# Another place of the heads in the transposed rows, merged early loads and another opening order in a retention + tanh-shrink kernel

## The chip, the cores and the metric

The kernel runs on one core of a Trainium2 chip. The metric is the device time of one execution in microseconds (us). Lower is better. The core has a matrix engine (TensorE, PE in the profile, with its weight loads as PEld), three engines for elementwise work (VectorE or DVE, ScalarE or ACT, GpSimd or POOL), and SyncE (SP), which here only issues DMAs. ScalarE can issue DMAs too. Each engine runs its own instructions in program order.

## The reference

Two blocks follow each other. The first is a recurrent retention over 4 batches, 8 heads, 768 tokens and head size 64, in float32:

```
gamma = 1 - 2 ** (-5 - arange(H));  scale = 1 / sqrt(D)
for t in range(S):
    state = gamma * state + outer(k[:, :, t], v[:, :, t])
    y[:, :, t] = scale * (q[:, :, t] @ state)
```

The second takes y as 3072 tokens of 512 features (8 heads x 64) and computes

```
h = x @ w_in            # 512 -> 2048
g = h - tanh(h)
out = g @ w_out         # 2048 -> 512
```

w_in and w_out come as float64 and are turned into float32 on the chip.

## The kernel before, in words

The 3072 tokens are 24 chunks of 128, six to a batch. A chunk ci passes these pieces, each with a letter in the order that is written out by hand (lines 891 to 912):

- Lk, Lq, Lv (`load_one`, line 245): the loads of its k, q and v, 256 KB each. The first eight chunks load q in another arrangement ("wide"), in two DMAs of 128 KB each (line 254). All go through SP's queue. There are two buffers for k, two for q, four for v, so a load waits until the earlier chunk in the buffer has been read.
- s, w (`scale`, line 266): q and v times powers of gamma, on VectorE (D) or POOL (P).
- t, T (`turn`, line 283): four transposes of k and four of q on TensorE into PSUM; c, C (`turn_copy`, line 301): ScalarE copies them out.
- p (`products`, line 331): 64x64 matmuls, k times v (line 342) and k times q (line 348); m (line 355): VectorE masks the scores; z, Z (lines 366 to 372): VectorE adds up the two states of the chunk.
- b (`outputs`, line 381), r: matmuls into the two y banks (line 397), b with the states and half of the masked scores, r with the other half; e (`see`, line 427): four tiny ScalarE reads between them; y (`keep_x`, line 443): ScalarE copies y into xT, the transposed rows that the second block uses as its input.

A 64x64 matmul uses one quarter of the array: a half of the rows (which half of the partitions it reads) and a half of the columns (which half it writes). Head h = 2p + i is pair p, member i. The place of its 64 output rows is set in `to_y`: before, the half of the columns is (i + p) % 2, the bank (ci + p) % 2. So in xT the heads of every second group of 128 rows stand swapped, and the rows of w_in are loaded in that order: in three DMAs (lines 126 to 135 and 159), one of 128 partitions and two of 64.

Weights come in 32 pieces of 512 KB (W): in each group of eight the first four are columns of w_in, the others rows of w_out. A piece is converted by A and l (ScalarE), D1 to D4 (VectorE), F and G (VectorE or POOL). The weights 3 to 8 are loaded into rooms that xT uses later.

The second block runs in steps of 256 tokens by 256 hidden features. A step has two halves of an up matmul (u, v; line 463), the activation (au, ath, aq0, aq1, alarge on ScalarE; f0 to f4 on VectorE) and a down matmul in two parts (o0, o1; line 530), with E for sums. The order covers chunks 0 to 7, weights 0 to 11 and steps 0 to 7. After it, loops run the remaining steps with the other chunks and weights between them; from the fifth group of 512 rows on by a form with fewer products (lines 668 and 777).

A piece "x:n" lets n dummy matmuls run ahead of the next TensorE group (`keep_busy`). Each engine and queue gets its instructions in the order in which the pieces are written, so a piece that waits holds up everything behind it on the same engine.

## Time and profile before

| | us |
|---|---|
| median of 4 runs (699.1 to 701.62) | 701.03 |
| profiled execution | 701.12 |
| its span | 699.3 |
| TensorE busy | 686.2 |
| VectorE busy | 520.0 |
| ScalarE busy | 433.2 |
| POOL busy | 350.3 |

The span goes from the first to the last instruction in the record; the execution's own time is 1.8 us longer. An engine counts as busy while one of its instructions runs. A line such as L342 is line 342 of the kernel. "A <- B x" in a table of waits says that A waited and B ended that wait. Idle time of an engine that is not the bottleneck costs nothing. The granted clock of TensorE was 1.00 throughout.

### The profile page before, as it was taken

How to read it: one execution, taken by the hardware profiler on the slowest of the kernel's cores; microseconds unless marked ns; L12 is line 12 of the kernel's file. 1: busy time of each engine (PE TensorE's matmuls, PEld its weight loads, DVE VectorE, ACT ScalarE, POOL GpSimd, SP SyncE). 2: the span in 40 equal slices, each digit the busy share in tenths (PEclk: the TensorE clock that was granted, in tenths of full speed). 3: DMA queues.
4: the chain of work that ended last, by engine and by line, in shares of the span. 5: the costliest groups of instructions: out<-in, count | busy, mean ns of one | idle time of the engine just before them, and what ended most of it. 6: DMA issues, size and time to landing. Idle time of an engine off the chain costs nothing.

```text
span 699.3 us, 16551 instructions
## 1 busy us (share of the span) xinstructions
PE 686.2 (98%) x6562; PEld 576.6 (82%) x6562; DVE 520.0 (74%) x893; ACT 433.2 (62%) x818; POOL 350.3 (50%) x518
## 2 busy tenths in 40 slices
PE   8889999999999999999999999999999999999997
PEld 7776666676767667789999999999999999999996
DVE  4787989988889865677776686676686676766765
ACT  4676777676866755565555665555566555566553
POOL 2352255554454685977854453354543444544333
PEclk9999999999999999999999999999999999999999
DMA  8883239878868666500000000000000000000001
GB/s 218 226 250 91 91 105 216 222 198 211 235 171 221 177 166 179 155 33 1 1 1 16 16 2 31 1 1 31 2 0 31 1 1 31 1 17 16 1 16 46
DMA packets 119677, 59.96 MB, mean 86 GB/s; under 512 B 101808, under 2 KB 112688, under 8 KB 119600
## 3 DMA queue, kind: packets, MB, share of 16 engines
q1 hardware_dynamic: 117008, 50.21, 27.9%
q10 hardware_dynamic: 2592, 8.69, 3.4%
q8 instruction: 52, 0.85, 0.5%
q14 instruction: 25, 0.20, 0.1%
HBM read 35.83 MB, written 14.68 MB: 72 GB/s over the span
## 4 chain that ended last, share of the span: by engine, by line
PE 92%; DMA 3%; DVE 1%; SPq 1%; issue 1%; ACT 1%; POOL 0%; POOLq 0%; DVEq 0%; ACTq 0%
PE h L777 28%; PE o L530 16%; PE h L463 15%; PE fast_t L668 10%; PE y L668 8%; PE fast_o L668 8%; PE y L397 3%; PE s L342 1%; PE s L348 1%; DMA raws<-in_moe_w_out_dram 1%; DMA k<-in_k_dram 1%; DMA v<-in_v_dram 1%; PE kqTp L297 1%; SPq L159 1%; SPq L254 0%
## 5 line engine op out<-in xcount | busy, mean ns | idle before, releaser
L476 ACT ACTIVATE th<-h 128x512 f32<-128x512 f32 x64 | 38.2, 597 | 142.2 <-DVE h L794 142.2
L619 POOL TENSOR_TENSOR s<-g 128x128 f32<-128x128 f32 x64 | 29.3, 457 | 191.5 <-DVE g L522 187.5
L463 PE MATMUL h<-xT,w 128*128 128x256 f32 x512 | 118.0, 382 | 0.0
L530 PE MATMUL o<-w,g 128*128 128x512 f32 x256 | 116.3, 596 | 0.0
L463 PEld LDWEIGHTS h<-xT,w 128*128 128x128 f32 x512 | 96.1, 190 | 22.2 <-issue 9.3
L530 PEld LDWEIGHTS o<-w,g 128*128 128x128 f32 x256 | 47.7, 190 | 46.5 <-issue 43.5
L777 PEld LDWEIGHTS h<-xT,w 128*128 128x128 f32 x512 | 76.8, 191 | 8.4 <-ACT fast_head L782 1.0
L522 DVE COPY_PREDICATED g<-large,th 128x512 f32<-128x512 int32 x88 | 72.3, 822 | 8.9
L777 PE MATMUL h<-xT,w 128*128 128x128 f32 x512 | 78.4, 276 | 0.2 <-ACT fast_head L782 0.2
L792 DVE TENSOR_TENSOR h<-h,fast_head 128x256 f32<-128x256 f32 x64 | 27.7, 432 | 67.7 <-PE h L777 65.1
L501 DVE TENSOR_TENSOR th<-h,th 128x512 f32<-128x512 f32 x88 | 60.1, 683 | 19.4 <-ACT th L474 18.2
L514 DVE SCALAR_TENSOR_TENSOR g<-q,h 128x512 f32<-128x512 f32 x64 | 44.1, 688 | 36.6 <-ACT q L490 35.3
L777 PE MATMUL h<-x,w 128*128 128x128 f32 x448 | 68.4, 275 | 0.0
L482 ACT ACTIVATE q<-u,tab 128x512 f32<-128x512 f32 x88 | 63.8, 725 | 1.7
L490 ACT ACTIVATE q<-u,tab 128x512 f32<-128x512 f32 x88 | 63.6, 723 | 0.0
L491 ACT ACTIVATE large<-u,tab 128x512 f32<-128x512 f32 x88 | 62.7, 712 | 0.0
L505 DVE SCALAR_TENSOR_TENSOR h<-q,h 128x512 f32<-128x512 f32 x88 | 60.8, 690 | 2.2 <-ACT q L482 2.2
L208 POOL TENSOR_TENSOR low<-low,power 128x512 f32<-128x512 f32 x25 | 32.5, 1298 | 56.6 <-DVE power L201 47.3
L777 PEld LDWEIGHTS h<-x,w 128*128 128x128 f32 x448 | 59.1, 192 | 0.0
L782 ACT COPY fast_head<-h 128x512 f32<-128x512 f32 x64 | 37.4, 585 | 19.5 <-PE h L777 18.8
L521 DVE TENSOR_TENSOR g<-g,u 128x512 f32<-128x512 f32 x64 | 48.0, 751 | 0.0
L787 POOL TENSOR_TENSOR fast_head<-fast_head 128x256 f32<-128x256 f32 x64 | 46.8, 731 | 1.5 <-ACT fast_head L782 1.5
(195 smaller groups left out, 1503.8 us busy)
## 6 DMA issues: line engine op xcount, KB each, us to landing
rows<-apart ACTq DMA_DIRECT2D x16, 512.0 KB, 4.2
k<-in_k_dram SPq DMA_DIRECT2D x24, 256.0 KB, 4.3
v<-in_v_dram SPq DMA_DIRECT2D x24, 256.0 KB, 5.7
raw<-in_moe_w_out_dram SPq DMA_DIRECT2D x12, 512.0 KB, 4.3
out_dram<-sum SPq DMA_DIRECT2D x22, 256.0 KB, 2.0
q<-in_q_dram SPq DMA_DIRECT2D x16, 256.0 KB, 4.7
raw<-in_moe_w_in_dram SPq DMA_DIRECT2D x14, 256.0 KB, 3.9
raw<-in_moe_w_in_dram SPq DMA_DIRECT2D x28, 128.0 KB, 4.0
```

The source lines that it names most:

```text
L463: nc.tensor.matmul(hp, w1[:, c, ts(2 * m2 + i, P)], xT[n // 2][:, c, ts(n % 2, TH)], start=(begins and c == 0), stop=(c == NC - 1), skip_g ...
L482: nc.scalar.activation(q0, shrinking[n, m2][0], AF.Square, bias=bias0)
L490: nc.scalar.activation(q1, u, AF.Square, bias=bias1, scale=math.sqrt(A))
L491: nc.scalar.activation(large, u, AF.Relu, bias=bias_m)
L501: nc.vector.tensor_tensor(th, hp, th, op=ALU.subtract)
L505: nc.vector.scalar_tensor_tensor(hp, in0=shrinking[n, m2][2], scalar=C0, in1=hp, op0=ALU.add, op1=ALU.mult)
L521: nc.vector.tensor_tensor(flat, src, u, op=ALU.mult)
L522: nc.vector.copy_predicated(flat, large.bitcast(I32), th)
L530: nc.tensor.matmul(o_p[j], gT[n, m2][:, i, ts(j, P)], w2[:, 2 * m2 + i], start=(first and i == 0), stop=(last and i == 1))
L668: nc.tensor.matmul(accs[n][k], left[k - 1], right, start=first and k in (1, 6, 7, 4), stop=last, skip_group_check=True)
L777: nc.tensor.matmul(hps[n, m2][:, ts(PLACE[k], P)], s_of[m2][k - 1][:, c], x_of[n][k - 1][:, c], start=(k == 1 and c == 0), stop=(c == 1), ...
L787: nc.gpsimd.tensor_tensor(odd_room[1], first[:, :2], first[:, 3:1:-1], op=ALU.add)
```

## The change

Four things change together.

1. The place of the heads: the half of the columns becomes p // 2, the bank (ci + i) % 2, the place in the bank p % 2. Every group of 128 rows in xT now holds one 64-row head of the first four and one of the last four, with no swap. The pieces of w_in are loaded in two DMAs of 64 partitions instead of three. The quarters of the array are walked in one fixed order, `QUARTERS`, in both parts of b and in r.
2. The wide q of the first eight chunks is loaded in one DMA of 256 KB instead of two of 128.
3. `load_one` takes a queue. Two loads, k of chunk 0 and q of chunk 1, are issued by ScalarE ("A" behind the number in the order).
4. The order of the opening is another: the loads of k, q and v of the first two chunks stand before weight 0, up steps come later, and other pieces are given to VectorE and POOL. The name of an o bank now carries n, since parts of different steps stand between each other.

```
--- before.py
+++ after.py
@@ -126,13 +126,8 @@
         f, r = divmod(i, 2 * NC)
         if r < NC:
             cols = ts(NC * f + r, P)
-            rows = w_in[:, cols].rearrange("(k two p) n -> p two k n", two=2, p=P)
-
-            return w1[:, :, cols], [
-                (ds(0, P), 0, rows[:, 0]),
-                (ds(0, D), 1, rows[D:, 1]),
-                (ds(D, D), 1, rows[:D, 1]),
-            ]
+            rows = w_in[:, cols].rearrange("(col c p) n -> col p c n", col=2, c=NC)
+            return w1[:, :, cols], [rows[0], rows[1]]
         m = NC * f + r - NC
         return w2[:, m], w_out[ts(m, P)]
 
@@ -155,8 +150,8 @@
             return
         if raw is not None:
             dst = raw.rearrange("p (c n) -> p c n", c=NC)
-        for r, k, w in src:
-            nc.sync.dma_start(out=dst[r, k::2], in_=w if raw is None else w.bitcast(U32))
+        for r, w in enumerate(src):
+            nc.sync.dma_start(out=dst[ts(r, D)], in_=w if raw is None else w.bitcast(U32))
 
 
 
@@ -242,7 +237,7 @@
     states = {}
     xT = {}
 
-    def load_one(ci, which):
+    def load_one(ci, which, queue=nc.sync):
         if ci >= NCH:
             return
         b, j = divmod(ci, CPB)
@@ -250,13 +245,12 @@
         t = inp.tile([P, H, D], F32, tag=nm, name=f"{nm}_{ci}", bufs=4 if nm == "v" else 2)
         rows = src[b, :, ts(j, P), :]
         if nm == "q" and ci < WIDE:
-            for i in range(2):
-                nc.sync.dma_start(
-                    out=t[:, ts(i, RUN)].rearrange("p r d -> p (r d)"),
-                    in_=rows[i::2].rearrange("g (p r) d -> p g (r d)", r=RUN),
-                )
+            queue.dma_start(
+                out=t.rearrange("p (i r) d -> p i (r d)", r=RUN),
+                in_=rows.rearrange("(g i) (p r) d -> p g i (r d)", i=2, r=RUN),
+            )
         else:
-            nc.sync.dma_start(out=t, in_=rows.rearrange("h p d -> p h d"))
+            queue.dma_start(out=t, in_=rows.rearrange("h p d -> p h d"))
         loaded.setdefault(ci, {})[which] = t
 
     def load_chunk(ci):
@@ -377,6 +371,7 @@
 
     y_banks = banks("y", "y").rearrange("p r (two n t) -> p two r n t", two=2, n=2)
     halfway = {}
+    QUARTERS = ((0, 0), (1, 1), (0, 1), (1, 0))
 
     def outputs(ci):
 
@@ -391,29 +386,24 @@
 
         def to_y(p, i, a, lhsT, rhs):
 
-            col, r = (i + p) % 2, (ci + p) % 2
+            col, r = p // 2, (ci + i) % 2
             start = (r, col) not in begun
             begun.add((r, col))
-            nc.tensor.matmul(y[ds(D * col, D), r, p // 2, ts(a, D)], lhsT, rhs,
+            nc.tensor.matmul(y[ds(D * col, D), r, p % 2, ts(a, D)], lhsT, rhs,
                              start=start, stop=True, skip_group_check=True)
 
         def intra(first):
-            for pp in range(NP // 2):
-                for i in range(2):
-                    for a in range(2):
-
-                        for col in range(2):
-                            p = 2 * pp + ((a + col) % 2 if first else (a + col + 1) % 2)
-                            if (i + p) % 2 != col:
-                                continue
-                            r = ds(D * a, D)
-                            to_y(p, i, a, vh[r, 2 * p + i], a_[r, i, p])
+            for odd in range(2):
+                for row, col in QUARTERS:
+                    p, i = 2 * col + odd, row if first else 1 - row
+                    r = ds(D * row, D)
+                    to_y(p, i, row, vh[r, 2 * p + i], a_[r, i, p])
 
         for a in range(2):
             if j or a:
-                for p in range(NP):
-                    for i in range(2):
-                        r = ds(D * i, D)
+                for odd in range(2):
+                    for i, col in QUARTERS:
+                        p, r = 2 * col + odd, ds(D * i, D)
                         to_y(p, i, a, st[r, a, p], qT[r, p, ts(a, D)])
         intra(True)
         halfway[ci] = intra
@@ -425,7 +415,7 @@
         for col in range(2):
             for r in range(2):
                 nc.scalar.copy(out=seen[ds(D * col, D), r : r + 1],
-                               in_=y[ds(D * col, D), r, 1, ds(D * ((ci + r + col) % 2), 1)])
+                               in_=y[ds(D * col, D), r, 1, ds(D * ((ci + r) % 2), 1)])
 
     def outputs_rest(ci):
         halfway.pop(ci)(False)
@@ -524,10 +514,10 @@
     def down(n, m2, j, first, last):
 
         if first:
-            o_p[j] = bank("o", f"o_{n}_{m2}_{j}")
-            keep_busy(o_p[j][:, :P])
+            o_p[n, j] = bank("o", f"o_{n}_{m2}_{j}")
+            keep_busy(o_p[n, j][:, :P])
         for i in range(2):
-            nc.tensor.matmul(o_p[j], gT[n, m2][:, i, ts(j, P)], w2[:, 2 * m2 + i],
+            nc.tensor.matmul(o_p[n, j], gT[n, m2][:, i, ts(j, P)], w2[:, 2 * m2 + i],
                              start=(first and i == 0), stop=(last and i == 1))
 
     def add_up(n, m2, j):
@@ -537,11 +527,11 @@
                 sums[i] = [op.tile([P, 2, DM], F32, tag="sum", name=f"sum_{i}"), set()]
         o, begun = sums[n][0][:, j], sums[n][1]
         if j in begun:
-            nc.vector.tensor_tensor(o, o_p[j], o, op=ALU.add)
+            nc.vector.tensor_tensor(o, o_p[n, j], o, op=ALU.add)
         elif done and j % 2:
-            nc.vector.tensor_copy(o, o_p[j])
+            nc.vector.tensor_copy(o, o_p[n, j])
         else:
-            nc.scalar.copy(out=o, in_=o_p[j])
+            nc.scalar.copy(out=o, in_=o_p[n, j])
         begun.add(j)
         if done:
             nc.sync.dma_start(out=rows_of(n)[:, j], in_=o)
@@ -853,11 +843,11 @@
             nc.vector.copy_predicated(gT[at_].rearrange("p i t -> p (i t)"),
                                       early[s, "large"].bitcast(I32), early[s, "th"])
 
-    engines = {"D": nc.vector, "P": nc.gpsimd}
+    engines = {"D": nc.vector, "P": nc.gpsimd, "A": nc.scalar}
     pieces = {
-        "Lk": lambda c: load_one(c, 0),
-        "Lq": lambda c: load_one(c, 1),
-        "Lv": lambda c: load_one(c, 2),
+        "Lk": lambda c, e=nc.sync: load_one(c, 0, e),
+        "Lq": lambda c, e=nc.sync: load_one(c, 1, e),
+        "Lv": lambda c, e=nc.sync: load_one(c, 2, e),
         "W": load_weights,
         "s": lambda c, e: scale(c, 0, e),
         "w": lambda c, e: scale(c, 1, e),
@@ -889,26 +879,26 @@
     if w_out.dtype != F32:
         rooms += [xp.tile([P, 2, 2 * BANK], U32, tag="xT", name=f"raws_{i}") for i in range(3)]
     order = """
-    Lk:0 Lq:0 Lv:0 x:9 t:0 s:0D Lq:1 x:3 T:0 W:0 w:0D Lk:1 c:0 C:0 A:0 x:2 p:0 z:0 Lv:1 m:0
-    Z:0 s:1P Lq:2 D1:0 D2:0 w:1D T:1 b:0 Lk:2 Lv:2 t:1 C:1 l:0 e:0 c:1 D3:0 r:0 x:2 p:1 W:1
-    D4:0 y:0 t:2 c:2 z:1 s:2P T:2 Lk:3 w:2P C:2 m:1 Z:1 b:1 p:2 e:1 r:1 F:0D A:1 G:0D D1:1 y:1
-    D2:1 z:2 Lq:3 Lv:3 Z:2 D3:1 l:1 W:2 s:3P x:1 t:3 w:3P u:0 m:2 Lq:4 c:3 T:3 s:4P C:3 D4:1
-    b:2 p:3 F:1D e:2 r:2 l:2 A:2 G:1D v:0 z:3 m:3 D1:2 y:2 Lv:5 Z:3 au:0 Lk:4 D2:2 D3:2 t:4
-    Lv:4 T:4 Lq:5 b:3 Lk:5 w:4P w:5D W:3 c:4 D4:2 F:2D C:4 e:3 W:4 W:5 ath:0 r:3 y:3 aq0:0
-    aq1:0 p:4 f0:0 z:4 m:4 Z:4 l:3 f1:0 A:3 alarge:0 u:2 G:2P t:5 s:5P T:5 v:2 D1:3 b:4 D2:3
-    D3:3 D4:3 A:4 c:5 F:3P f2:0 C:5 l:5 ath:2 Lq:6 Lk:6 Lv:6 W:7 e:4 G:3P Lq:7 W:8 W:9 p:5
-    au:2 Lv:7 r:4 aq0:2 y:4 A:5 aq1:2 l:4 f3:0 u:1 f0:2 m:5 z:5 f4:0 s:6P t:6 W:6 w:6P T:6
-    Lk:7 W:10 v:1 W:11 s:7P b:5 f1:2 f2:2 f3:2 c:6 C:6 au:1 p:6 e:5 D1:5 D1:4 D2:5 D2:4 r:5
-    D3:5 aq1:1 alarge:2 alarge:1 aq0:1 ath:1 u:3 D3:4 D4:5 v:3 D4:4 F:5P z:6 m:6 F:4D Z:6 f0:1
-    G:4D au:3 T:7 G:5P t:7 f1:1 A:6 y:5 c:7 f2:1 D1:6 o1:0 f4:2 w:7P C:7 b:6 D2:6 f3:1 p:7
-    aq0:3 e:6 ath:3 r:6 l:6 v:4 u:4 D3:6 m:7 f0:3 f1:3 D4:6 z:7 F:6P G:6P y:6 l:7 alarge:3
-    aq1:3 f2:3 f3:3 A:7 D1:7 b:7 f4:1 o0:0 A:11 e:7 D2:7 D3:7 D4:7 F:7P G:7D u:5 r:7 v:5 o1:1
-    o0:1 ath:4 au:4 aq0:4 l:11 f0:4 f4:3 f1:4 l:9 aq1:4 f2:4 f3:4 D1:11 E1:1 alarge:4 A:9 D1:9
-    D2:9 D2:11 D3:9 E0:1 y:7 ath:5 au:5 aq0:5 aq1:5 alarge:5 o1:2 v:7 D3:11 D4:11 o0:2 o1:3
-    D4:9 u:7 F:9D G:9P f0:5 o0:3 f1:5 F:11D f2:5 f3:5 f4:4 f4:5 G:11P A:8 D1:8 D2:8 E1:3 D3:8
-    Z:7 au:7 l:8 A:10 D1:10 D4:8 l:10 aq1:7 D2:10 F:8D D3:10 ath:7 f0:7 aq0:7 E0:3 D4:10 u:6
-    v:6 o0:4 au:6 o1:4 F:10P f1:7 f2:7 ath:6 alarge:7 G:10P f0:6 aq1:6 aq0:6 f1:6 alarge:6
-    o0:5 o1:5 E0:5 f3:7 f2:6 Lv:8 f3:6 f4:7 f4:6 Lk:8 Lq:8 W:12 W:14 W:13 G:8P E1:5
+    Lq:0 Lv:0 s:0P Lk:0A w:0D Lq:1A x:9 t:0 T:0 Lk:1 C:0 c:0 x:2 p:0 s:1P Lv:1 t:1 T:1 Lq:2
+    z:0 m:0 Z:0 Lv:2 C:1 W:0 w:1D c:1 b:0 Lk:2 Lq:3 x:1 p:1 s:2D e:0 z:1 m:1 r:0 y:0 Z:1 A:0
+    T:2 l:0 x:1 b:1 x:1 t:2 C:2 e:1 D1:0 c:2 D2:0 w:2P D3:0 Lk:3 Lv:3 x:1 p:2 r:1 D4:0 s:3P
+    m:2 y:1 z:2 t:3 Z:2 T:3 W:1 C:3 c:3 b:2 Lq:4 F:0P G:0P e:2 A:1 W:3 Lk:4 w:3D p:3 z:3 D1:1
+    r:2 y:2 l:1 Z:3 m:3 D2:1 u:0 D3:1 b:3 D4:1 e:3 Lv:4 F:1D s:4P r:3 T:4 A:3 x:1 t:4 G:1D v:0
+    Lq:5 D1:3 D2:3 y:3 c:4 C:4 l:3 w:4D p:4 D3:3 W:2 Lv:5 D4:3 Lk:5 s:5P z:4 m:4 au:0 ath:0
+    u:2 Z:4 Lq:6 T:5 F:3P w:5P W:4 aq0:0 v:2 A:2 Lv:6 t:5 C:5 D1:2 G:3P aq1:0 alarge:0 Lk:6
+    Lq:7 W:5 c:5 b:4 f0:0 p:5 D2:2 f1:0 D3:2 l:2 s:6P f2:0 D4:2 e:4 A:4 f3:0 m:5 D1:4 r:4
+    ath:2 v:1 z:5 t:6 au:2 T:6 aq0:2 aq1:2 c:6 y:4 l:4 F:2P C:6 G:2P u:1 A:5 Lk:7 W:7 Lq:8 W:6
+    w:6P f0:2 W:8 D2:4 Lv:7 f1:2 D3:4 s:7P f2:2 b:5 p:6 f4:0 f3:2 W:9 D1:5 W:10 D4:4 e:5 D2:5
+    F:4P W:11 z:6 m:6 r:5 Z:6 u:3 au:1 D3:5 alarge:2 aq0:1 D4:5 l:5 aq1:1 F:5D ath:1 T:7 G:4D
+    A:6 l:6 t:7 c:7 y:5 G:5D f0:1 v:3 f1:1 f4:2 f2:1 ath:3 f0:3 o1:0 au:3 C:7 f3:1 D1:6 D2:6
+    D3:6 o0:0 b:6 w:7P aq1:3 e:6 aq0:3 alarge:1 f1:3 D4:6 p:7 m:7 F:6P r:6 f2:3 v:4 alarge:3
+    y:6 u:4 A:7 au:4 z:7 f3:3 G:6D D1:7 f4:1 D2:7 D3:7 D4:7 b:7 u:5 v:5 A:9 l:7 F:7D G:7D e:7
+    r:7 o1:1 aq0:4 aq1:4 ath:4 A:8 D1:9 E1:1 o0:1 o0:2 au:5 l:9 D2:9 D3:9 f0:4 f1:4 f2:4 f3:4
+    D4:9 D1:8 f4:3 aq1:5 E0:1 alarge:4 y:7 ath:5 D2:8 D3:8 f4:4 F:9D G:9P f0:5 l:8 aq0:5 o1:2
+    D4:8 F:8P u:7 o0:3 f1:5 A:10 G:8P D1:10 f2:5 A:11 f3:5 v:7 au:7 D2:10 D1:11 o1:3 E0:3
+    D3:10 aq0:7 ath:7 l:10 D4:10 f0:7 f1:7 D2:11 F:10D E1:3 alarge:5 f4:5 D3:11 v:6 G:10D u:6
+    aq1:7 alarge:7 au:6 aq0:6 D4:11 f2:7 f3:7 f4:7 aq1:6 ath:6 o0:4 l:11 F:11P f0:6 f1:6
+    alarge:6 Z:7 f2:6 f3:6 f4:6 o1:4 o0:5 o1:5 Lk:8 Lv:8 W:12 W:13 W:14 E0:5 G:11P E1:5
     """
     for piece in order.split():
         kind, at_ = piece.split(":")
```

## The prediction

> **What bounds the kernel now.** I read the page's shares first, then the table of stretches, then what TensorE waits for, then SP's queue.
>
> ```profile
> PE 686.2 (98%) x6562; PEld 576.6 (82%) x6562; DVE 520.0 (74%) x893; ACT 433.2 (62%) x818; POOL 350.3 (50%) x518
> PE 92%; DMA 3%; DVE 1%; SPq 1%; issue 1%; ACT 1%; POOL 0%; POOLq 0%; DVEq 0%; ACTq 0%
> ```
>
> TensorE is busy 98% of the span and carries 92% of the chain. A change that leaves its work alone can win only what it idles.
>
> ```profile
> 0.00:10.00 10.00, 8.90 (x120) 8.34 (x120) 2.58 (x6) 2.45 (x3) 1.25 (x5) 1.00 0.83 208
> 10.00:20.00 10.00, 7.55 (x245) 6.40 (x246) 7.49 (x15) 5.81 (x19) 2.44 (x2) 1.00 0.92 231
> 30.00:40.00 10.00, 7.42 (x196) 6.34 (x190) 5.92 (x11) 6.36 (x13) 5.73 (x5) 1.00 0.94 263
> 50.00:60.00 10.00, 8.57 (x143) 6.55 (x142) 8.57 (x16) 7.38 (x19) 3.35 (x4) 1.00 0.87 232
> 60.00:70.00 10.00, 10.00 (x96) 6.62 (x95) 7.86 (x13) 5.87 (x14) 3.54 (x3) 1.00 0.00 0
> ```
>
> Columns: stretch, length, busy us of PE, weight load, VectorE, ScalarE, POOL, granted clock, DMA share, GB/s. With 8.90 and 9.77 in the two rows left out, TensorE idles 8.9 us in the first 60 us and not at all in the next ten. So the opening (the order written out by hand) is where the change can count. The DMA engines are 76 to 94% busy there: bytes, not SP's issuing, limit the loads once they run.
>
> ```profile
> PE kqTp L297 <- DMA k<-in_k_dram: 1.8, 2, 1.4
> PE y L397 <- ACT seen L427: 1.7, 3, 0.8
> PE s L342 <- ACT kqT L306: 1.6, 1, 1.6
> PE y L397 <- issue: 1.1, 1, 1.1
> PE kqTp L232 <- DVE w L116: 1.1, 1, 1.1
> PE s L342 <- POOL v L281: 1.0, 1, 1.0
> ```
>
> Waits in the opening: total, times, longest. No single cause: late loads (chunk 7's k, chunk 4's v), the copies out of PSUM and the first memset.
>
> ```profile
> 0.73 0.45 SPq L259 DMA_DIRECT2D k<-in_k_dram  x1
> 1.24 1.29 SPq L254 DMA_DIRECT2D q<-in_q_dram  x2
> 6.65 0.59 SPq L259 DMA_DIRECT2D k<-in_k_dram  x1
> 7.29 1.12 SPq L259 DMA_DIRECT2D v<-in_v_dram  x1
> 46.93 0.38 SPq L259 DMA_DIRECT2D k<-in_k_dram  x1
> ```
>
> Chunk 1's k and v are issued only at 6.65 and 7.29 us, chunk 7's k at 46.93.
>
> **The loads.** Eight q loads lose one issue each and eight w_in loads of the opening one each. At about 0.6 us (1.29 for two q) that is 16 x 0.6 = 9.6 us of SP's time. Packets and bytes stay, so I price it at nothing: the DMA engines, 76 to 94% busy, cover it. Without that cover it could win part of the 9.6 us. The other end is a loss of 0.3: a q half landed after 3.3 us at best, a 256 KB load after 3.6, and one scaling waits for each. Two loads go to ScalarE's queue at 1.2 to 2.4 us. ScalarE's first copy ran at 6.15, so they cost it nothing; they also pass SP's queue, so q1 is issued near 1.8 instead of 3.21 and k1 (SP) near 2.0 instead of 6.65. The Trainium skill (DMA: Bandwidth & Descriptors, Issuing engines are not separate DMA queues) says that issuing from several engines saves only sequencer time. By that rule this edit is worth nothing and only the new order counts. By the rows the two loads take 1.3 us of issuing out of SP's way at the start, and I let that count through k1 and v1 below.
>
> **The place of the heads.** It makes as many matmuls as before, in another order of quarters, with neighbouring quarters in two PSUM banks instead of one. Chunk 5's 32 state matmuls start 0.51 us before the next group (45.71 to 46.22), the 32 of L342 0.46 (46.46 to 46.92). So 24 x 0.05 = 1.2 us either way bounds it. I take zero, as groups of 16 for L397 already run at 0.24, the rate of L342.
>
> **The order, by hand.** Rates from the trace: one transpose group (t, T) 0.45 us, products (p) 0.94, outputs (b) 0.86, their rest (r) 0.23, half an up step (u, v) 1.73 to 1.92; VectorE 0.69 for 512 elements and 0.42 for 256; POOL 1.04 for a scaling and 1.28 for F or G; ScalarE 0.59 a copy, 0.45 for the four small reads (e), 0.65 for y. I step through the new order engine by engine.
>
> Start. The first 8 us moved 22, 197, 309, 219, 295, 300 and 281 GB/s after the first idle one. Tables and q0 go first now, so k0 ends after 0.87 MB instead of 0.44: it lands near 6.0 instead of 4.3. The nine dummies last until 4.85, so TensorE stands 1.2 us. t0 and T0 end at 7.5, the two copies at 8.9, p0 at 9.4, against 8.9 before: 0.5 lost. VectorE then does z0, m0, Z0 and w1 by 11.7; k1 (8.0) and v1 (9.1, at worst 11) are there. p1 ends at 12.7, against 14.73: 2.0 ahead.
>
> Next, r0, T2, b1 and t2. ScalarE has y0, A0, l0 before C2, e1, c2, which end at 16.75; p2 waits 0.9 us for that and ends at 17.25. t3, T3 and b2 follow. w3 on VectorE ends at 19.7, p3 at 20.7, r2 at 20.95. Weight 0 has passed F and G on POOL by 19.1, ahead of its use; u0 runs from 20.95 to 22.9. Before, the same set (chunks 0 to 3 up to p3, r2, u0) ended at 25.39: 2.5 ahead.
>
> Then b3, a wait of 0.65 for e3, r3, T4, t4, v0 (weight 1 ready at 26.0), p4, u2, T5, v2, t5, b4, p5 run to 35.1. Before, p5 began at 39.27 and ended at 40.3: 5 ahead. Chunk 4's v has landed near 24 instead of 29.9. p5 no longer follows ScalarE's six other items, but still its own copy.
>
> Up to b7, TensorE's work adds 18.7 us (five halves 8.65, two o 3.44, four transposes 1.8, p6 and p7 1.9, b5 to b7 2.4, r4 to r6 0.5): 53.8. VectorE has the later end. After z5 (done at 37.2) it has 32 instructions up to z7,, 19.3 us at full durations: z7 at 56.5, b7 0.9 later, 57.4. Before, b7 ended at 61.99, with equal work done (one up half more, one o less). That is 4.6 ahead. Two things that my table lacks stood in the trace: an issue wait of 1.08 at 17.98 and collisions of VectorE with POOL.
>
> ```profile
> 14.15 1.15 DVE L201 TENSOR_SCALAR power<-head 128x512 uint32<-128x512 uint32 x1
> 28.59 0.42 DVE L201 TENSOR_SCALAR power<-head 128x512 uint32<-128x512 uint32 x1
> ```
>
> I subtract 1.1 for the first and count the second in the range: 4.6 - 1.1 = 3.5 us. Loads behind waits stay hidden. SP stands at k6 until p4 has read k4 (28.5), and at k7 until p5's reads (34.6); behind k7 are W5's successors W7, q8, W6, W8, v7. v7 lands near 46 and p7 wants it at 50: 3 us of cover, and past that each us late costs one.
>
> **The sum.** The profiled execution took 701.12 us, 1.8 over its span of 699.3, and stands 0.09 over the median of 701.03. 701.03 - 3.5 = 697.5.
>
> **Rivals.** First, slower: VectorE becomes the bound of the opening. Both orders give it 27 two-operand steps before z7, but the new one would have z7 at 56.5 where it was at 59.46. A collision costs 0.73 (1.15 against 0.42), on either side. From five more of them VectorE loses the lead of 3.5; eight give 8 x 0.73 - 3.5 = +2.3, 703.4. For it: POOL gets 19 operations before z7 instead of 17, and VectorE is 86% busy from 40 to 60. Against it: VectorE's neighbours overlap (57.32, 57.93 and 58.53 are starts of 0.69 us instructions), worth up to 2.4 us on the 19.3.
>
> Second, the lead is given back: VectorE is busy 17.57 of 20 us from 80 on and 18.93 from 100 on, so TensorE, ahead by 3.5, would wait for it there. Its idle time from 60 to 100 is 5.6 us. If all but 0.5 of the lead is eaten the time is 700.5.
>
> Third, the pace at the start. TensorE's weight loads took 230 ns up to 5.5 us and 139 from 6.7 on. With a stand of 1.2 us at 4.85 the slow pace may start over; 5.6 us of it from 6.0 on would double t0 to b0, some 3.9 us, of which waits hide 1.8. That leaves a gain of 3.5 - 2.1 = 1.4: 699.6. The Trainium skill (TensorE: Matmul & The Clock Gate, Part 1) speaks against this gap: it wants about 3.4 us of steady work, in a window that runs free, before full pace. By that rule the gap adds between nothing and 3.4 us at half pace, at most 1.7 us.
>
> Fourth, the loads don't come earlier in effect. Without the 2.0 us at p1 and the 1.4 of k7's wait, 3.5 - 3.4 = 0.1 is left: 700.9.
>
> **How the numbers follow.** Forecast 0.60, its own range 693.8 (TensorE's own end at b7, 53.8, with 1.1 off) to 698.9. VectorE bound and slower: 0.24. Lead given back, slow pace or loads no earlier: 0.16 together, 699.6 to 700.9, all within 0.3% but for a little at the edge. A measurement tells about 0.3% (2.1 us) from no change. So faster 0.62, same 0.14, slower 0.24. The range leaves out more than half of the slower case (0.14) and a little below: 693.6 to 702.6.
>
> **What would show it.** Right: p1 ended near 12.7 us, u0 near 22.9, p5 near 35 to 37, b7 near 58; TensorE's idle in the first 60 us at about 5 to 6 us; no wait for chunk 7's k; busy time per matmul as before; the first stretch without idle beginning some 3 us earlier. Wrong: TensorE waits behind m or z of chunks 5 to 7, v7 landing after 50, weight loads of 230 ns past 7 us, or a different time for L397's matmuls in all 24 chunks.

## The result, and the profile after

| | before | after |
|---|---|---|
| median, us | 700.58 (78 runs) | 701.94 (53 runs) |
| lowest to highest, us | 698.83 to 703.63 | 699.29 to 705.92 |
| profiled execution / its span, us | 701.12 / 699.3 | 704.2 / 702.3 |

Ratio after to before: 1.002, 95% interval 1.0012 to 1.0028. The change costs 1.4 us (a difference that lies inside 0.3%), where 3.5 us of gain were forecast. Medians of the kernel before differ between chips by up to 0.7 us, so each experiment below is held against the kernel before on its own chip.

The profiled execution of after is one of its longer ones: 704.2, 2.3 us over the median. So what its profile shows below explains a loss of 3 us, not of 1.4; two more profiles of the same kernel, after_again and after_third, stand beside it further down.

The page after, the engines' row and the chain's shares by engine:

```profile
PE 688.2 (98%) x6560; PEld 578.3 (82%) x6560; DVE 523.8 (75%) x894; ACT 433.1 (62%) x818; POOL 347.7 (50%) x517
PE 94%; DVE 2%; issue 2%; DMA 1%; ACT 1%; POOL 0%; POOLq 0%; SPq 0%; DVEq 0%; ACTq 0%
```

TensorE has the same work but is busy 2 us longer. The table of stretches of after (columns as in the prediction: stretch, length, busy PE, weight load, VectorE, ScalarE, POOL, granted clock, DMA share, GB/s):

```profile
0.00:10.00 10.00, 7.27 (x96) 6.74 (x97) 1.68 (x3) 2.36 (x3) 2.29 (x6) 1.00 0.92 228
10.00:20.00 10.00, 7.58 (x184) 6.36 (x182) 6.18 (x12) 4.14 (x15) 3.25 (x3) 0.83 0.80 196
20.00:30.00 10.00, 7.98 (x225) 6.81 (x224) 4.78 (x10) 4.52 (x13) 3.39 (x4) 0.83 1.05 242
30.00:40.00 10.00, 9.38 (x167) 7.91 (x166) 8.15 (x14) 5.67 (x14) 4.38 (x5) 1.00 0.80 197
50.00:60.00 10.00, 10.00 (x176) 7.25 (x171) 9.73 (x19) 7.80 (x19) 2.61 (x2) 1.00 1.09 261
```

The row of before from 20 to 30 us, to hold beside it:

```profile
20.00:30.00 10.00, 8.90 (x224) 7.56 (x222) 8.70 (x15) 6.48 (x20) 3.53 (x3) 1.00 0.76 196
```

Two things are new: the granted clock of 0.83 from 10 to 30 us, which was 1.00 in the profile before, and less work for VectorE and ScalarE in these 20 us (VectorE 11.0 us busy, before 16.2). TensorE's waits in the opening of after, total, times and longest:

```profile
PE s L336 <- issue: 2.1, 2, 1.6
PE y L227 <- issue: 1.9, 1, 1.9
PE s L342 <- issue: 1.8, 1, 1.8
PE s L336 <- DVE v L275: 1.7, 2, 1.3
PE kqTp L227 <- DVE w L116: 1.1, 1, 1.1
PE y L392 <- ACT seen L417: 0.6, 1, 0.6
PE kqTp L291 <- DMA k<-in_k_dram: 0.4, 1, 0.4
```

The profile counts two matmuls for each f32 matmul of the kernel, and so do the numbers here. L227 are dummies, L291 the transposes, L336 and L342 the products k times v and k times q, L392 the outputs, L453 the up matmuls. The long waits for chunk 4's v and chunk 7's k that the profile before had are gone. In their place stand two waits of 1.86 and 1.85 us put down to "issue": none of the releases that the profile shows came late. (The 1.6 on L336 is chunk 5's products and has another cause, below.) The second of the two in TensorE's timeline of after (start, length, line, form; the last bracket is the idle time ahead):

```profile
24.20 0.67 PE L342 MATMUL s<-kqT 64*64 64x64 f32 x29
26.71 0.37 PE L342 MATMUL s<-kqT 64*64 64x64 f32 x2 [1.85 <-issue]
27.55 3.22 PE L453 MATMUL h<-xT,w 128*128 128x256 f32 x8
```

TensorE stops inside a group of 32 matmuls, after the 29th; all 32 wait for the same data, so it isn't data that is late. The eight up matmuls behind it take 3.22 us, where eight of them took 1.89 to 2.00 in the profile before. Before had two such stops, shorter ones, the second in the same products:

```profile
19.06 0.45 PE L397 MATMUL y<-a,v 64*64 64x64 f32 x12 [1.08 <-issue]
24.69 0.40 PE L348 MATMUL s<-kqT 64*64 64x64 f32 x13 [0.45 <-issue]
25.32 1.99 PE L463 MATMUL h<-xT,w 128*128 128x256 f32 x8
```

The stretches that tell why the up matmuls took longer, of after:

```profile
16.41:19.82 3.41, 3.11 (x55) 2.69 (x55) 1.51 (x3) 0.91 (x6) 2.02 (x2) 0.50 0.73 187
26.65:30.06 3.41, 3.35 (x25) 2.78 (x25) 2.80 (x6) 1.21 (x3) 1.02 (x1) 0.50 1.11 256
```

From the end of each of the two stops on (0.30 and 0.06 us ahead of it), TensorE's clock is granted at half for 3.41 us.

What did the opening of this execution lose as a whole? From about 80 us on the two profiles run alike: the rows of 16 up matmuls that start at 81.54 before and 84.49 after both lie 617.8 us ahead of their span's end. So the 2.95 us between these rows are the whole difference of the spans. Up to them TensorE idles 9.86 us after and 8.88 before, from the gaps between its matmuls: +0.98. This is 3.7 us of such stops in place of 1.5 (1.08 and 0.45 before), and 6.2 us of all other waits in place of 7.4. The other 2.0 us are the same work at half clock: the up matmuls take 1.1 us more, the outputs 0.6, the dummies 0.7 (32 of them, 34 before), the rest 0.4 less.

The two other profiles of after have no half clock in the opening. Their rows start at 80.74 (after_again) and 81.06 (after_third): 0.8 and 0.5 us ahead of before, with 1.5 and 2.9 us of stops. So at full clock these two show a small lead in the opening; with one profile of before to compare, that is an indication. After_again loses it later. From that row on it takes 619.9 us in place of 617.8, and its table of waits has a line that before and after don't have, for a load of a later chunk, at 176 us:

```profile
PE s L342 <- DMA kqT<-rows: 1.6, 1, 1.6
```

The same wait stands in profiles of the old order (0.99 us in before_few4, below), so the new order isn't what brings it.

How often is the clock at half? An execution with one such stretch has a mean granted clock of 0.998 or less. In the runs below, 80 of 127 executions of before are at 0.9985 or more, with a median of 699.8, and the other 47 at 700.3. Of after's own 54 executions only 22 are, at 700.5; the other 32 are at 703.1. With after_again and after_third it is 36 of 76. The change has more executions with half clock, and these lose more by it (2.6 us, before 0.5); at full clock the medians are still 0.6 us apart (0.9 with all 36), and where this part comes from stays open.

### The profile page after: what moved, and what is told of

Same layout as the page of the kernel before. It is cut to its first block, busy times and chain, and to the rows that moved or that the text cites. A ratio compares the mean times of both kernels' runs of the same rounds, so it can differ in the third digit from the quotient of the medians.

```text
span 702.3 us, 16491 instructions
## 1 busy us (share of the span) xinstructions
PE 688.2 (98%) x6560; PEld 578.3 (82%) x6560; DVE 523.8 (75%) x894; ACT 433.1 (62%) x818; POOL 347.7 (50%) x517
## 4 chain that ended last, share of the span: by engine, by line
PE 94%; DVE 2%; issue 2%; DMA 1%; ACT 1%; POOL 0%; POOLq 0%; SPq 0%; DVEq 0%; ACTq 0%
PE h L767 28%; PE h L453 16%; PE o L520 16%; PE fast_t L658 10%; PE y L658 8%; PE fast_o L658 8%; PE y L392 3%; PE s L336 2%; PE s L342 2%; DMA v<-in_v_dram 1%; PE kqTp L291 1%; DMA k<-in_k_dram 1%; DVE v L275 0%; DVE g L512 0%; DVE g L504 0%
## 5 line engine op out<-in xcount | busy, mean ns | idle before, releaser
L453 PE MATMUL h<-xT,w 128*128 128x256 f32 x512 | 119.2, 385 | 0.0
L453 PEld LDWEIGHTS h<-xT,w 128*128 128x128 f32 x512 | 96.9, 192 | 22.0 <-issue 9.3
L512 DVE COPY_PREDICATED g<-large,th 128x512 f32<-128x512 int32 x88 | 74.1, 842 | 8.9
L203 POOL TENSOR_TENSOR low<-low,power 128x512 f32<-128x512 f32 x27 | 35.1, 1301 | 56.0 <-DVE power L196 28.4
```

Of the source, the lines that this page charges most:

```text
L453: nc.tensor.matmul(hp, w1[:, c, ts(2 * m2 + i, P)], xT[n // 2][:, c, ts(n % 2, TH)], start=(begins and c == 0), stop=(c == NC - 1), skip_g ...
L512: nc.vector.copy_predicated(flat, large.bitcast(I32), th)
```

## The experiments

The theories, as the expectations name them. **A**: TensorE runs out of instructions in the dense runs of small matmuls, and its clock falls behind such a stop. **B**: the place of the heads or the larger loads cost time. **C**: the chain of VectorE and ScalarE in the new order costs it. **D**, formed later: the new order has no lead to lose.

### One half of the change at a time

**e_layout**: after's place of the heads, loads of w_in and wide q, before's order, all loads on SP. Against after:

```
-    Lq:0 Lv:0 s:0P Lk:0A w:0D Lq:1A x:9 t:0 T:0 Lk:1 ...
+    Lk:0 Lq:0 Lv:0 x:9 t:0 s:0D Lq:1 x:3 T:0 W:0 ...
```

> The old order with the new place of the heads, w_in in two DMAs and the wide q in one; nothing on ScalarE's queue. Theory A (the new order packs chunks 0 to 3 so tightly that TensorE runs out of instructions, the issue waits of 1.86 and 1.85 us, and its clock then falls to half for a while): the place and the merged loads are not at fault, so the time stays within 0.5 us of before, and the issue waits of the opening stay at the 1.5 us of before. Theory B (the new place or the larger loads hold something up): about 1.4 us slower than before, as the changed kernel is. Theory C (the lead is lost to VectorE and ScalarE in the new order): as A here.

**e_order**: before, with after's order, ScalarE's two loads and the o banks' names; heads, w_in and q as before. Against after:

```
-            col, r = p // 2, (ci + i) % 2
+            col, r = (i + p) % 2, (ci + p) % 2
...
-            queue.dma_start(
+            for i in range(2):
+                queue.dma_start(
...
```

> The new order, with the two loads on ScalarE's queue, on the old place of the heads, three DMAs for w_in and two for the wide q. Theory A: issue waits near 1.9 us twice and half clock in part of the executions, as in the changed kernel; 1 to 3 us slower than before. Theory B: no slower than before, since the place is the old one. Theory C: slower by 1 to 3 us, but with the granted clock at 1.000 and the waits on VectorE or ScalarE.

Measured: e_layout 699.24 beside 699.72, ratio 1.001 (0.9989 to 1.0031); e_order 699.81, ratio 1.0009 (0.9998 to 1.0021). By the medians neither half is slower than before, where the whole costs 1.4 us. But both intervals reach the whole's ratio of 1.002, so this pair doesn't settle the theories. It speaks against C. A's number for e_order (1 to 3 us slower) was missed and B's was met; for e_layout A's time was met, but its stops add up to 3.2 us, not 1.5. The profile of e_order has its stop at the same matmul of the same group as after, but it is short, and no half clock follows:

```profile
21.96 0.68 PE L348 MATMUL s<-kqT 64*64 64x64 f32 x29
23.26 0.27 PE L348 MATMUL s<-kqT 64*64 64x64 f32 x2 [0.63 <-issue]
23.76 1.99 PE L463 MATMUL h<-xT,w 128*128 128x256 f32 x8
```

e_layout's executions fall apart: six at a mean granted clock of 0.9985 or more with a median of 698.6, six below with 703.3. Its profile has half clock from 32.07 to 35.49, behind a stop of 1.34 us.

**e_late_u**: before, with one up half moved behind the run of small matmuls, which gets denser by it.

```
-    ... x:1 t:3 w:3P u:0 m:2 ... b:2 p:3 F:1D e:2 r:2 l:2 ...
+    ... x:1 t:3 w:3P m:2 ... b:2 p:3 F:1D e:2 r:2 u:0 l:2 ...
```

> The kernel before with one edit: the first up half (u of step 0) is moved behind the rest of chunk 2, so that T3, b2, p3, r2 follow each other as in the new order. Theory A: a new issue wait of 0.5 to 2 us before u, in some executions a granted clock under 1.000, and 0 to 2 us slower than before. Theory C: the same work on TensorE with T3 to r2 2 us earlier for VectorE and ScalarE, so no slower, 0 to 0.5 us faster.

Measured: 699.78, ratio 1.0001 (0.9993 to 1.001). So in the old order a denser run alone costs nothing that shows: its stops in the profile were 0.58, 0.80 and 0.42 us. Both theories' ranges take this in.

### Where the stops come from

The page lists a queue "instruction" beside the queues of the data. In the page of after:

```profile
q8 instruction: 52, 0.85, 0.5%
```

These are 52 packets of 16 KB; with 6560 matmuls and 6560 weight loads that is one packet for about 252 of TensorE's instructions. The kernels of the last group of experiments, with 364 or 480 fewer matmuls and as many fewer weight loads, have 49 and 48 packets, again one for about 253. The profile counts their time in the same 16 DMA engines as that of the loads. Against them, all stops of over 0.3 us that the profile puts down to "issue" inside a group, with times in us. "Place" is the number of TensorE's records (matmuls, weight loads and a few others) that started ahead of the resuming matmul:

```
kernel         stop   place   resumes at   last packet ended   later by
before         1.08    706    19.06        17.64               1.42
before         0.45    961    24.69        23.32               1.37
after          1.86    449    16.71        15.33               1.38
after          1.85    961    26.71        25.12               1.59
after_again    1.54    961    23.80        22.40               1.40
after_third    1.14    449    15.93        14.64               1.29
after_third    0.43    706    19.83        18.38               1.45
after_third    1.37    961    24.46        23.05               1.40
e_order        0.63    961    23.26        22.03               1.23
e_layout       1.44    706    18.57        17.12               1.45
e_layout       0.45    961    24.20        22.72               1.49
e_layout       1.34   1217    31.24        29.79               1.44
e_late_u       0.58    706    18.03        16.48               1.55
e_late_u       0.80    962    23.46        21.98               1.48
e_late_u       0.42   1474    37.38        35.88               1.50
e_split        1.69    961    23.95        22.38               1.57
e_less         1.20    706    18.92        17.50               1.42
e_less         1.99    961    24.16        22.56               1.61
e_sp           0.89    706    20.24        18.96               1.28
e_sp           3.02    961    26.51        25.14               1.37
e_layout_act   0.77    706    17.80        16.26               1.55
e_layout_act   1.82    961    24.81        23.34               1.47
e_layout_act   3.93   1217    35.03        33.85               1.19
```

Every one of the 23 stops ends 1.2 to 1.6 us after a packet. And all stand at five places, 449, 706, 961, 1217 and 1474, which are 255 to 257 records apart, as the borders between packets of about 256 would be, whatever the order of the pieces. Of the other waits of over 0.3 us in the opening only one, in e_fill (below), stands within 10 records of such a place. So these are waits for TensorE's own instructions.

Why is one long and another short? At the place 961 before and after differ in the run, not in the packet. The packet begins 2.67 us after TensorE passes the place 706 in before, 2.73 in after. But the 255 records between the two places take TensorE 5.18 us in before, with an up half among them, and 3.55 in after. Elsewhere the packet is late by itself: in e_layout_act it begins 7.93 us after the place 961, and the stop is 3.93. The packets last 0.9 to 2.0 us while loads run, no longer ahead of long stops than of short ones. In after the DMA engines' share is 1.05 in the stretch of the second stop; around it (23.5 to 26 us) the loads' queue takes all of it:

```profile
q1 hardware_dynamic: 1978, 0.54, 103.7%
q8 instruction: 1, 0.02, 2.7%
```

That the loads are what holds up a packet fits this, but isn't shown.

### Loads cut again, taken away, or moved

**e_split**: after, its wide q in two DMAs again and each w_in piece in four.

```
-            nc.sync.dma_start(out=dst[ts(r, D)], in_=w if raw is None else w.bitcast(U32))
+            for c in range(0, NC, 2):
+                nc.sync.dma_start(out=dst[ts(r, D), c : c + 2], ...)
```

**e_less**: after, 1 MB of w_in's first four pieces not loaded; POOL sets it to zero.

```
+            if i < 4 and r:
+                nc.gpsimd.memset(raw[ts(r, D)].bitcast(F32), 0.0)
+                continue
```

**after_again** is after, unchanged, on the same chip as these and e_sp.

> The changed kernel with its loads cut smaller: the wide q in two DMAs as before, each w_in half in two (four per weight). Bytes and packets stay. Theory A in the form that larger DMAs let SP queue more bytes ahead of the instruction packets: fewer late packets, fewer executions at lower clock, 1 to 2 us faster than the changed kernel. If the late packets don't depend on how SP cuts the loads: within 0.7 us of the changed kernel. If SP's issuing is what the opening waits for: slower by up to 1 us.

> The changed kernel with 1 MB of loads left out: of weights 0 to 3 only the first 64 partitions are loaded, the others are set to zero by POOL, so the output is not the reference's. TensorE's work is the same. Theory A: with fewer bytes queued from 8 to 25 us the instruction packets come in time, issue waits fall under 1 us in all, the clock stays up: 1.5 to 3 us faster than the changed kernel. Theory C: nothing waits for those bytes, and POOL has four operations more: no faster, up to 0.5 us slower.

> The changed kernel once more, beside the next three on one chip. In its first profile TensorE stood 1.86 and 1.85 us for instructions (the 16 KB instruction packets began at 14.0 and 24.0 us, after 445 and 884 of TensorE's instructions, where the other five profiles have them after 224 to 276 and 758 to 789) and ran at half clock for 3.4 us twice. Theory A (instructions late behind the loads, then half clock): a second profile shows late packets again, at other places, or none, and the time follows: about 700 without, 702 to 704 with. Theory C (the order itself is slower by waits on VectorE and ScalarE): the same waits in the same places and 701 to 702.

Measured: after_again 701.86, ratio 1.002 (1.0003 to 1.0037); e_split 701.3, ratio 1.0016 (1.0001 to 1.0031); e_less 700.21, ratio 1.0007 (0.9996 to 1.0017). How SP cuts the loads doesn't decide. A megabyte less gives 1.65 us by the medians, though the stops in its profile stay (1.20 and 1.99 us), at full clock. Its row near 80 us starts at 80.96, after_again's at 80.74, so these two profiles don't show the gain in the opening. A's time was met and its waits were not; by which way the bytes matter stays open.

**e_sp**: after, the two loads on SP again.

```
-    Lq:0 Lv:0 s:0P Lk:0A w:0D Lq:1A x:9 ...
+    Lq:0 Lv:0 s:0P Lk:0 w:0D Lq:1 x:9 ...
```

> The changed kernel with k of chunk 0 and q of chunk 1 issued by SP again. k then is issued third on SP, near 2.2 us instead of 1.14, and what follows is 1.2 us later at the start. Theory A: no change in the later stalls, up to 0.7 us slower. If two queues at once are what delays TensorE's instructions: no late packet at 14 us, no half clock after it, 1 to 2 us faster.

Measured: 704.37, ratio 1.006 (1.0043 to 1.0077). In this order the loads on ScalarE's queue are a gain of 2.5 us (701.86 of after_again, same chip), more than either expectation had. In e_sp's profile TensorE waits 0.94 us for chunk 0's k and then stays at its slow pace up to 10.3 us: four transposes take 1.06 us there, and 0.60 in after's profile. Then comes a stop:

```profile
26.51 0.27 PE L342 MATMUL s<-kqT 64*64 64x64 f32 x2 [3.02 <-issue]
```

Half clock follows it from 27.33 to 30.74.

**e_layout_act**: e_layout, the same two loads on ScalarE's queue.

```
-    Lk:0 Lq:0 Lv:0 x:9 t:0 s:0D Lq:1 x:3 ...
+    Lk:0A Lq:0 Lv:0 x:9 t:0 s:0D Lq:1A x:3 ...
```

> The kernel with after's place of the heads and merged loads but before's order, and now also the two loads (k of chunk 0, q of chunk 1) on ScalarE's queue. If two loads on ScalarE's queue are worth 2.5 us by themselves, as their removal from the kernel after showed: 697 to 698. If what they are worth comes from the place of chunk 0's k behind tables and q on SP in the new order alone: 699 to 699.8, as the kernel with before's order and no ScalarE queue. Theory B (place or larger loads cost time): over 701.

Measured: 701.98, ratio 1.0014 (0.9997 to 1.0032). No gain in the old order; by the median it is even over 701, as B had it, with an interval that takes in no change. Two executions at 0.9985 of the clock or more have a median of 698.7, the ten others 702.2; its profile has stops of 1.82 and 3.93 us and half clock from 33.49 to 40.32.

### Filling the run, or breaking it up

**e_fill**: after, 12 more dummies in the dense run.

```
-    T:2 l:0 ... z:2 t:3 Z:2 T:3 W:1 C:3 c:3 b:2 ...
+    x:4 T:2 l:0 ... z:2 x:4 t:3 Z:2 T:3 W:1 C:3 c:3 x:4 b:2 ...
```

> The changed kernel with twelve more dummy matmuls ahead of T of chunk 2, t of chunk 3 and b of chunk 2 (four each, 0.27 us apiece by the trace of before, 3.2 us in all). Theory A: they fill time in which TensorE would stand without instructions and keep its clock up, so the issue waits shrink by as much as the dummies add and no execution falls to half clock: 1 to 2 us faster than the changed kernel, level with before. Theories B and C: 3.2 us of work more on TensorE, so 2 to 3 us slower than the changed kernel, 704 to 705.

**e_early_u**: after, the up half ahead of chunk 2's outputs. **after_third** is after once more, beside it.

```
-    ... C:3 c:3 b:2 Lq:4 F:0P G:0P e:2 ... D2:1 u:0 D3:1 ...
+    ... C:3 c:3 F:0P G:0P u:0 b:2 Lq:4 e:2 ... D2:1 D3:1 ...
```

> The kernel after with one up half (u of the first step, 8 matmuls, 2.0 us) moved from behind chunk 3's rest to ahead of chunk 2's outputs, so that it breaks up the dense run of small matmuls (turns of 3, outputs of 2, products of 3), and F and G of weight 0 ahead of it in the text (G ended at 21.5 us in the profile after, the outputs of 2 began at 22.6). No work is added or left out. Theory A (TensorE runs out of instructions in the dense run, because its third packet of instructions is late there): the issue wait of 1.5 to 3.0 us in the products of chunk 3 shrinks to under 0.8, and the time is 1 to 2 us under that of the kernel after on this chip: 700 to 701. If the late packet only shows up in a later place: stall elsewhere, time as after, 701.5 to 702.2. Theories B (place of the heads, larger loads) and C (the chain of VectorE and ScalarE in the new order): as after, within 0.5.

> The kernel after, unchanged, on this chip beside the two others: 701.5 to 702.2 by the earlier runs. Its profile should show an issue wait of 1.5 us or more in the products of chunk 3 again, ended 1.3 to 1.7 us after the end of an instruction packet.

Measured: e_fill 704.4, ratio 1.0071 (1.0055 to 1.0088); e_early_u 702.32, ratio 1.0043 (1.0026 to 1.006); after_third 702.16, ratio 1.0043 (1.0023 to 1.0063). Theory A's numbers were missed twice. The stop in chunk 3's products went in both, but a row of e_early_u and one of e_fill show what came instead:

```profile
21.11 1.99 PE L453 MATMUL h<-xT,w 128*128 128x256 f32 x8 [2.07 <-POOL w L212]
```

```profile
51.70 0.68 PE L291 MATMUL kqTp<-tab,wide 128*128 128x128 f32 x4 [3.37 <-DVE w L212]
```

In e_early_u the up half waits 2.07 us for weight 0, which POOL has not finished. In e_fill, besides 3.2 us of dummies, TensorE stands for 3.37 us at 48 us, and half clock follows. The profile names VectorE's weight there, which ended 0.69 us before TensorE resumed; but a packet ended 1.65 us before it, and the place is 1985, 511 records (two packets) behind 1474. So this too is a wait for instructions, moved to a later border. Both kernels lost the stop in chunk 3's products at a price, so neither tells what it costs. After_third's own stop there was 1.37 us (1.5 or more was expected).

### Fewer instructions at the same work

**before_few**, **after_few**: in chunks 1 to 7 the 32 products of k and v (16 in the kernel's own count) as four of 128x128 by 256 columns (two in the kernel's count), and in chunks 1 to 5 and 7 the states' outputs likewise.

```
+        few = 1 <= ci < WIDE
+        for a in range(2 * few):
+            nc.tensor.matmul(halves[:, a, 1].rearrange("p n t -> p (n t)"),
+                             kh[:, ds(2 * a, 2)].rearrange("p h d -> p (h d)"),
+                             vh[:, ds(NP, NP)].rearrange("p h d -> p (h d)"),
+                             start=True, stop=True, skip_group_check=True)
+        for p in range(0 if few else NP):
...
```

> The kernel before, with fewer instructions for TensorE in the opening at about the same busy time: in chunks 1 to 7 the 32 products of k and v (64x64) become two of 128x128 by 256 columns, and in chunks 1 to 5 and 7 the 32 of states and q become two of the same size. (Eight of 128x256 took 1.99 us in the up step, so two take 0.5, as the 32 small ones did.) Each chunk then has 76 matmuls for TensorE instead of 136, with the same inputs, outputs and waits; heads are mixed, so the output is not the reference's. This is the base for the next kernel: 699 to 701 by every theory, some 0.5 less by theory A, as two or three short issue waits of 0.4 to 1.4 us go.

> The kernel after with the same replacement, chunks 1 to 7; the output is not the reference's. Theory A (TensorE's instructions come too late in the dense runs of small matmuls, and the stalls lower its clock): no issue wait of over 0.8 us up to 30 us but the one at the copy of chunk 5, no half clock before 100 us, and the new order keeps the lead that it earns: 1.5 to 3.5 us under the kernel before with the same replacement. Theory C (the chain of VectorE and ScalarE in the new order costs the time) and theory B (the place of the heads and the larger loads cost it): the difference between the two stays what it is with the small matmuls, 1.4 to 2.2 us over.

Measured: before_few 701.25, ratio 1.0019 (1.0009 to 1.0029); after_few 703.55, ratio 1.0053 (1.0039 to 1.0066). The stops and the half clock went in both profiles, and yet after stayed 2.3 us behind, which is near what B and C had expected. But a group took 1.06 us in place of 0.51 (the expectation took the kernel's two for two of the eight that the profile counts in an up half; they are four there), so TensorE had 5.4 us more work up to the row near 80 us, and the waits that the two orders differ in were mostly covered (idle up to that row 4.46 and 5.55 us). The 1.1 us of idle time is about half of the 2.3; the other half stays open. The pair doesn't decide; the next three do better.

**before_few4**, **after_few4**, **layout_few4** (e_layout): four matmuls of 64x64 by 256 columns for each 16 by 64 (the kernel's count), the same columns streamed in each quarter.

```
+        few = 1 <= ci < WIDE
+        for a in range(2 * few):
+            for i in range(2):
+                r = ds(D * a, D)
+                nc.tensor.matmul(halves[ds(D * i, D), a, 1].rearrange("p n t -> p (n t)"),
+                                 kh[r, 6 + i], vh[r, ds(NP, NP)].rearrange("p h d -> p (h d)"),
+                                 start=True, stop=True, skip_group_check=True)
...
```

(k times q and the states' outputs in the same way.)

> The kernel before with fewer instructions for TensorE in the opening, at the same streamed columns: in chunks 1 to 7 four matmuls of 64x64 weights by 256 columns take the place of 16 by 64 columns, in each half of the products, and in the states' part of the outputs of chunks 1 to 5 and 7. The last pair of this sort used 128x128 weights, whose two took 1.06 us in place of 0.51, so that TensorE got 5.4 us more work and waits were hidden; here a group should take 0.5 as before. Heads are mixed, so the output is not the reference's. By every theory some 0 to 2 us under the kernel before (two or three issue waits of 0.5 to 1.1 us can go): 698 to 700.5.

> The kernel after with the same replacement; the output is not the reference's. Theory A (late instructions, and half clock behind the stalls, took the whole lead of the new order): no issue wait but that of chunk 5's copy, and 1.5 to 3.5 us under the kernel before with this replacement. Theory D, new, from the last pair (both without issue waits, and the new order still idled 1.1 us more): the new order earns no lead even without stalls, since other waits stand where the old ones stood: within 0.7 of the kernel before with this replacement, or slower. Theory B (place of the heads and larger loads) is told from D by the third kernel.

> The kernel with after's place of the heads and larger loads in before's order (the earlier e_layout), with the same replacement; the output is not the reference's. Theories A and D: 0 to 1.2 us under the kernel before with this replacement, as the undisturbed executions of the order with small matmuls. Theory B: over it by as much as the kernel after with this replacement.

| | median, us | ratio to before, interval |
|---|---|---|
| before, same chip | 700.35 | |
| before_few4 | 699.15 | 0.9972 (0.996 to 0.9985) |
| after_few4 | 698.12 | 0.9974 (0.9963 to 0.9986) |
| layout_few4 | 698.6 | 0.9968 (0.9955 to 0.9981) |

With fewer instructions the kernel after goes from 0.2 to 0.4% above before to 0.26% under it; the kernel before gains 0.28%. The slowdown of the change is gone with the small matmuls, as theory A has it, and B is out, as the three agree; only the walk of the quarters in the states' outputs isn't tested here, since the replacement takes it out. But the lead over before_few4 is 1.0 us by the medians and none by the ratios, not the 1.5 to 3.5 of theory A: D holds for most of it. Of 12 executions of after_few4, 11 are at 0.9985 of the clock or more; of before_few4 6 of 11, of layout_few4 8 of 11.

Half clock doesn't need a late packet, though. The profile of before_few4 has no stop inside a group, but this wait for the load of chunk 1's k, and half clock around it:

```profile
12.15 1.09 PE L297 MATMUL kqTp<-tab,k 128*128 128x128 f32 x4 [1.44 <-DMA k<-in_k_dram]
11.51:18.34 6.83, 6.19 (x47) 4.43 (x48) 3.80 (x8) 1.93 (x9) 2.44 (x2) 0.50 0.80 209
```

In layout_few4's profile it runs from 38.87 to 42.28, 2.06 us after a wait of 1.40 us for ScalarE's copy. After_few4's waits in the opening:

```profile
PE s L336 <- issue: 2.6, 2, 1.6
PE kqTp L227 <- DVE w L116: 1.1, 1, 1.1
PE s L342 <- ACT kqT L303: 0.9, 1, 0.9
PE y L408 <- ACT seen L442: 0.6, 1, 0.6
```

No stop inside a group is left. The 2.6 us of L336 are the products of chunks 5 and 7, whose waits are put down to "issue" too, but stand ahead of a whole group. For chunk 5 the timelines of after_few4, TensorE's and then ScalarE's, point to the cause:

```profile
37.23 0.66 PE L336 MATMUL s<-v,k 64*64 64x256 f32 x8 [1.60 <-issue]
```

```profile
35.32 0.72 ACT L850 ACTIVATE q<-u,tab 128x512 f32<-128x512 f32 x1
35.94 0.71 ACT L850 ACTIVATE large<-u,tab 128x512 f32<-128x512 f32 x1
36.55 0.57 ACT L303 COPY kqT<-kqTp 128x512 f32<-128x512 f32 x1
```

The products start 0.11 us after the end of the copy of chunk 5's k, which stands behind two activations. In the code they write the PSUM banks that this copy reads (both have the tag "t" from chunk 4 on), so they have to wait for it. Chunk 7 has the same with its copy of q (it ends at 54.55, the products start at 54.65 after 0.96 us), and so has the profile of after for chunk 5 (43.63 and 43.73, after 1.57 us). This part is what C named, a wait on ScalarE. What it would give to move that copy ahead has no measurement, and e_layout has no second one; its executions at full clock have the lowest median of the kernels with all the small matmuls (698.6).

## Why the prediction was wrong

**Loads.** Right in sign and kind. Chunk 7's k and chunk 4's v are no longer waited for, so the fourth rival (loads no earlier) falls. Cut and size of the DMAs cost nothing that shows (e_split). The ScalarE queue is worth some 2.5 us in the new order (e_sp), more than the 1.3 us of issuing that the rows gave, and nothing in the old one (e_layout_act). The Trainium skill's sentence (DMA: Bandwidth & Descriptors, Issuing engines are not separate DMA queues), that only sequencer time is saved, speaks of the direct saving. Here 704.37 against 701.86 came with a slow start up to 10.3 us and a stop of 3.02 us in e_sp's profile, so what a load waits for can cost more than the time saved.

**Place of the heads.** Zero fits: the groups of L392 take 0.69 and 0.41 us, the times of L397 before, and layout_few4 is like before_few4. e_layout's 1.001 (0.9989 to 1.0031) is too wide to confirm the bound of 1.2 us.

**Start.** About right. k0 landed at 5.6 (forecast 6.0), p0 ended at 9.8 (9.4), because VectorE's scaling of v0 took 1.45 us beside POOL's of q1 and TensorE waited 1.31 for it; p1 ended at 13.3 (12.7), 1.4 us ahead of before. The third rival's slow pace behind the wait for k0 didn't come in the three profiles of after. But it was real: in e_sp it lasted up to 10.3 us, in e_split, behind a wait of 1.00 us for q0's scaling, up to 10.5.

**The marks behind it.** Here it failed:

```
end of                      p1     u0     p5     b7     start of the row near 80 us
forecast                    12.7   22.9   35.1   57.4
before                      14.7   25.4*  40.3   62.0   81.5
after                       13.3   30.7   44.7   66.6   84.5
e_order                     13.3   25.7   39.7   62.0   79.9
after_few4                  12.2   23.7   38.1   60.4   78.3
* the set of chunks 0 to 3 up to p3, r2, and u0; all ends to within 0.2
```

First, "an issue wait of 1.08", of which "I subtract 1.1", was the failed step. I took the wait for a loss that stays as it is. It is a packet of instructions that comes late, and what it costs depends on the order: where the run between two borders gets denser, a packet as late stops TensorE for longer (1.85 us in place of 0.45 at the place 961). The three profiles of after have 3.7, 1.5 and 2.9 us of stops; before has 1.5, and I had counted 1.1. In the first of them 2.0 us of work at half clock come on top. Where the instructions come in time, in after_few4, u0 ends at 23.7, 0.8 us from the forecast.

Second, "p5 no longer follows ScalarE's six other items, but still its own copy" was followed by no price. That copy stands behind two activations and holds p5 for 1.57 to 1.60 us in the profiles of the new order (1.17 in after_few). After_few4 reaches p5 3.0 us later than forecast: 0.8 of it stood at u0 already, 1.6 is this wait. At b7 it is 3.0 still.

Third, I counted wrong between p5 and b7: the order has six up halves there, not five. TensorE's own end would be 55.5 us, not 53.8; VectorE's 57.4 stays the later one, so only the low end of the range rests on the slip. And the work at b7 isn't equal: both orders have done ten up halves, but the new one has done one o that before does later, 1.7 us more. This hid part of the lead: put right, it would have made the forecast still lower.

Fourth, I compared the new order with an old order that pays for its own late instructions. Freed of them, the old order gains 1.2 us (before_few4). So of 3.5 us of lead, after_few4 shows 2.2 over before, and 1.0 or less over before_few4.

**Rivals.** VectorE as the bound: not what made it slower. It is 9.73 of 10 us busy from 50 to 60, but TensorE's table has no wait for m or z of chunks 5 to 7. The lead given back in the main loop, by waits for VectorE: no. From the row near 80 us on, nine of fifteen profiles, before and after among them, take 617.8 to 618.0 us, and e_split 618.2. The five others take 618.5 to 619.9, each with a wait for a later chunk's "kqT<-rows", in both orders. The slow pace: right in kind; in after's profile it stands behind the stops at 16 and 27 us instead of behind the wait for k0. The Trainium skill (TensorE: Matmul & The Clock Gate, Part 1) asks for a whole idle window of some 3.4 us before the clock falls. Here it fell behind stops of 1.86, 1.85 and 1.34 us; its window of 3.41 us agrees.

What stays open: why the packets of the table begin anywhere from 1.3 to 7.9 us after TensorE has passed the border before. More load on the DMA engines at that time is the likeliest, but e_less, which took load away, kept its stops. Open too is why after has more executions with half clock than before.

## What to carry to other kernels

Read a wait that the profile puts down to "issue" inside a group of like instructions against the packets of the instruction queue, and count at which instruction it stands: in runs of small matmuls TensorE's own instructions can come late, and making the runs tighter can cost there what it wins. Before a dependency wait is booked as won, follow the next instruction on the other engines' queues to the copy it really needs. Compare two orders both with their stops taken out, or the old order's own losses are booked as the new one's gain. And where executions of one kernel differ by more than the change, as here, look at several profiles of it: the first of after shows 3 us of loss, two others a small lead in the opening.

## What the runs showed that I had not expected

- TensorE resumes 1.2 to 1.6 us after the end of a 16 KB packet of about 256 instructions, at the same count of its instructions in every kernel with all the small matmuls here (449, 706, 961, 1217, 1474); the packets last 0.9 to 2.0 us while loads run, and the stops were 0.4 to 3.9 us.
- Half clock for 3.41 us (or twice that) follows a stop of as little as 1.34 us, but not every one: after_again's 1.54 and e_less's 1.99 had none. It follows other waits as well: 1.44 us for a load, 1.40 for a copy.
- f32 matmuls with 128x128 weights by 256 columns took twice the time (1.06 us for two, 512 columns) of 16 with 64x64 weights by 64 columns in four quarters (0.51, 256 columns in each quarter) for the same number of results; four with 64x64 weights by 256 columns took 0.48.
